# One load queue, a rewritten opening order, and earlier slots for turns and gates, in a recurrence-plus-feed-forward kernel

## The chip, the cores and the metric

The kernel runs on one core of one Trainium2 chip. The metric is the device time of one execution in microseconds (us). Runs are taken in rounds beside runs of the kernel before on the same chip. A ratio is the mean time of one kernel's fast runs over the mean of the other's fast runs of the same rounds. It is therefore not quite the ratio of the two medians that are quoted with it. The brackets after a ratio are its 95% interval.

The kernel before took 401.45 us (three runs, 400.94 to 402.1).

## The reference, cut to what matters

```python
def _attn_ref(x, f_logit, lower_bound):            # x, f_logit: (4, 6144, 256)
    sig = 1.0 / (1.0 + np.exp(-f_logit))
    f = lower_bound + (1.0 - lower_bound) * sig
    i = 1.0 - f
    for t in range(S):                              # a gated recurrence along the sequence
        h = f[:, t] * h + i[:, t] * x[:, t]
        y[:, t] = h

def _moe_ref(x, w1, w2, w_out):                     # 24576 tokens, 256 -> 1024 -> 256
    return np.maximum(x @ w1, x @ w2) @ w_out
```

The kernel uses max(a, b) = a + relu(b - a). The hidden products use the difference of the two weights, and the part that is linear in `x @ w1` becomes one 256x256 product (`w13` in the code).

## The kernel before: the parts that matter

There are 48 blocks of 512 tokens. Blocks 0 to 3 (the "opening") are loaded as plain rows and transposed on TensorE. All later blocks go another way, in chunks of two. POOL starts a DMA that casts both inputs to bf16 in DRAM ("cast"). SyncE (SP) then starts DMA transposes of them into SBUF ("turn"). Then ScalarE (ACT) makes the gate and VectorE (DVE) the drive, the forget factors and the scans ("gate").

```python
    def turn_dma(c):                                  # chunk c = blocks 4+2c, 5+2c
        for s, name in enumerate(("fs", "xs")):
            t = ttpool.tile([P, KC, CB * TB], BF16, name=("fT", "xT")[s])
            turned[c, s] = t
            nc.sync.dma_start_transpose(out=t[:], in_=spare[c % NS, name][:])

    def cast_behind(c):
        if c + 1 < NCH:
            last = CB * TB - 1                        # POOL waits here for the transpose fT
            nc.gpsimd.tensor_copy(out=held[:], in_=turned[c, 0][:, KC - 1, last : last + 1])
            cast(c + 1)

    def gate(j):                                      # ACT
        ...
        nc.scalar.activation(out=us[j][:], in_=part(j, 0), func=AF.Sigmoid, scale=-1.0)

    def drive(j):                                     # DVE; forget_half and scan_half follow
        nc.vector.tensor_tensor(out=vs[j][:], in0=us[j][:], in1=part(j, 1), op=ALU.mult)
```

The order of the opening is a hand-made list of items. Each item is one instruction group. Its suffix names the engine: `.a` ACT, `.v` DVE, `.p` POOL. `H` is a hidden product, `R` its relu, `P` a projection step, `G`/`V`/`F`/`S` are gate, drive, forget and scan, `TU`/`TV` transposes on TensorE, `D`/`SC` weight difference and scale, `warm` filler matmuls, and `CA` the first cast and turn. `O` copies a finished output out; the other letters round, transpose and apply weights. In the list of loads, `f0a` is half a of block 0's gate input, `x0a` that of its other input, and `w13` quarter 3 of w1 (not the product of the same name). Each engine works through its own part of the list in order.

```python
    LOADS = """
    f0a x0a f0b w13 w23 x0b w12 w22 wo3 w11 w21 w10 wo2 w20 f1a x1a wo1 f1b wo0 x1b
    f2a x3b f3a x2a f2b x2b f3b x3a
    """
    PLAN = """
    warm1 keeps_T G0a RW3.p V0a keeps TU0a D30.p F0a1.v G0b warm1 TV0a warm3 TU0b
    F0a0.a S0a1 F0b0.a warm1 TW3 S0a0 F0b1.a KW3.a V0b SC30.a D31.p RW2.v D20.p
    ...
    P150 R27.a H22a P160 H23a R22.a S3b0 H25b H25a H20b H23b H20a R25.a R23.v R20.v
    P120 O11.v O10.a
    """
    turn_of = {(4, 1): 1, (6, 0): 2}
    turn_of |= {(NP + c * CB - 3, 5): c for c in range(3, NCH)}
    gate_of = {(3, 3): 4, (4, 0): 5, (5, 0): 6, (5, 5): 7, (6, 6): 8, (7, 3): 9}
    gate_of |= {(b - 2, 5): b for b in range(10, NBLK)}
    ...
        for k, name in enumerate(LOADS.split()):
            load_item(name, nc.scalar if k in (1, 3) else nc.sync)   # x0a alone goes to ACT's queue
            if k == 0:
                nc.sync.dma_start(out=lbr[:], in_=lower_bound...)
    ...
        for j in range(3, NBLK + 1):
            for fc in range(FC):                      # slot (j, fc), eight in a block
                if j < NBLK:
                    hidden(j, fc)                     # two 128x512 matmuls, then relu(j, fc) on ACT
                project(j - 1, fc)                    # five 128x256 matmuls
                if fc == 0 and j > 3: store(j - 2, 1) # copy on DVE, then the store's issue on SP
                if fc == 4 and j < NBLK: store(j - 1, 0)
                ...
                if (j, fc) in gate_of:  ...           # gate, drive, forget, scan of a later block
                if (j, fc) in turn_of:  ...           # turn of a chunk, cast of the next
```

Slot (0) of block j needs the relus of slots 0 to 4 of block j-1.

Of the kernel before, what the change touches and what calls it, by code (L numbers as in the profile page):

```python
# [12 lines left out]
P = 128  # L13
# [3 lines left out]
def kernel(  # L17
# [13 lines left out]
    nc = tc.nc  # L31
# [26 lines left out]
    midpool = ctx.enter_context(tc.tile_pool(name="mid", bufs=2))  # L58
    ypool = ctx.enter_context(tc.tile_pool(name="ypool", bufs=4))
    rpool = ctx.enter_context(tc.tile_pool(name="rpool", bufs=3 * FC))  # L60
    opool = ctx.enter_context(tc.tile_pool(name="opool", bufs=6))
    lastpool = ctx.enter_context(tc.tile_pool(name="last", bufs=2))
    PS = bass.MemoryType.PSUM
    ps_d = ctx.enter_context(tc.tile_pool(name="ps_d", bufs=5, space=PS))
# [28 lines left out]
        ffs[j] = nffpool.tile([P, KC, TB], BF16, name="nff")  # L93
        ys[j] = ypool.tile([P, KC, TB], BF16, name="y")

    def load(j, s, q0, q1, eng=nc.sync):
        src = (f_logit, x)[s]
        eng.dma_start(
            out=ins[j][s][:, q0:q1, :],
            in_=src[0, j * TB + q0 * P : j * TB + q1 * P, :].rearrange(  # L100
                "(q p) d -> p q d", p=P
            ),
        )
# [128 lines left out]
    def relu(j, fc, on_dve=False):  # L232
        rt = rpool.tile([P, TB], BF16, name="rt")
        rts[j, fc] = rt
        if on_dve:
            nc.vector.tensor_relu(out=rt[:], in_=dts[j, fc][:])
        else:
            nc.scalar.activation(out=rt[:], in_=dts[j, fc][:], func=AF.Relu)  # L238

    def hidden(j, fc):  # L240
        dts[j, fc] = ps_d.tile([P, TB], FP32, name="dT")
        for kc in range(KC):
            nc.tensor.matmul(  # L243
                dts[j, fc][:],
                lhsT=wd[:, kc, unit(fc)],
                rhs=ys[j][:, kc, :],
                start=(kc == 0),
                stop=(kc == KC - 1),
            )
        relu(j, fc)  # L250

    pos = {}
# [90 lines left out]
    def wout_load(k):  # L343
        nc.sync.dma_start(
            out=won[:, 2 * k : 2 * k + 2, :],
            in_=moe_w_out[k * QF : (k + 1) * QF, :].rearrange("(q p) c -> p q c", p=P),
        )
# [90 lines left out]


    LOADS = """  # L440
    f0a x0a f0b w13 w23 x0b w12 w22 wo3 w11 w21 w10 wo2 w20 f1a x1a wo1 f1b wo0 x1b
    f2a x3b f3a x2a f2b x2b f3b x3a
    """
    PLAN = """
    warm1 keeps_T G0a RW3.p V0a keeps TU0a D30.p F0a1.v G0b warm1 TV0a warm3 TU0b
    F0a0.a S0a1 F0b0.a warm1 TW3 S0a0 F0b1.a KW3.a V0b SC30.a D31.p RW2.v D20.p
    warm5 TV0b S0b0 D21.p D11.p S0b1 TW2 KW2.v SC31.a H07a SC21.v H06a RO3.a warm3
    H07b H06b SC20.a R07.a W133 H05a D10.v H05b R06.a RW0.a H04b SC10.v P071 SC11.v
    H04a RW1.p P060 P061 R05.v D00.v H02b RO2.p TW0 R04.a H02a R02.a G1a D01.p TW1
    RO1.p P040 H03b KW0.v KW1.a SC00.v P051 SC01.v H03a V1a R03.a W132 P070 TU1a  # L450
    P041 H01b H00b H01a TV1a G1b F1a1.v H00a P030 P020 P031 R00.a RO0.p W131 TU1b
    P021 F1a0.v S1a1 W130 R01.a P050 F1b0.a S1a0 G2a P010 KL1.a V1b TV1b KL0.a
    F1b1.v P000 TU2a H11a H14a H16a S1b1 G3a P001 S1b0 P011 L01 F2a1.a H11b V2a H14b
    L00 F2a0.v H17a G2b O01.a R14.v TV2a L11 R11.a H16b L10 TU2b S2a0 R16.a G3b P140
    H17b S2a1 H12a H12b P141 F2b1.v P111 R17.a H13b V2b H13a H15a R12.a F2b0.v H15b
    TV2b P170 TU3b CA H10b H10a R15.a R13.v P110 F3b1.a TU3a R10.a F3b0.a S2b1 P121
    P130 S2b0 V3a P151 H21a H21b F3a1.a P161 H26b H26a R21.a TV3a P100 V3b H24a
    F3a0.v R26.a P131 S3a1 H24b H27b P171 H22b TV3b R24.a H27a P101 O00.a S3a0 S3b1
    P150 R27.a H22a P160 H23a R22.a S3b0 H25b H25a H20b H23b H20a R25.a R23.v R20.v
    P120 O11.v O10.a  # L460
    """

    engines = {"a": nc.scalar, "v": nc.vector, "p": nc.gpsimd}

    def load_item(name, eng=nc.sync):
        if name[0] == "w":
            k = int(name[2])
            if name[1] == "o":
                wout_load(k)
            elif name[1] == "1":  # L470
                weight_load(k, w1n, moe_w1)
            else:
                weight_load(k, w2n, moe_w2)
        else:
            half = 2 * "ab".index(name[2])
            load(int(name[1]), "fx".index(name[0]), half, half + 2, eng)

    outs = []

# [5 lines left out]
    def issue(item):  # L485
        name, _, e = item.partition(".")
        eng, on_dve, on_act = engines.get(e), e == "v", e == "a"
        kind = name.rstrip("0123456789ab")
        arg = ["ab".index(c) if c in "ab" else int(c) for c in name[len(kind) :]]
        if kind == "warm":  # L490
            keep_warm(arg[0])
        elif name == "keeps_T":
            turn_bound()
        elif name == "keeps":
            keeps()
        elif kind in ("G", "V") and len(arg) == 2:
            (gate_nat if kind == "G" else drive_nat)(arg[0], 2 * arg[1], 2 * arg[1] + 2)
        elif kind in ("TU", "TV"):
            turn_pe(arg[0], "UV".index(kind[1]), arg[1])
        elif kind == "F" and len(arg) == 3:  # L500
            j, x, h = arg
            tok = slice(x * HB, (x + 1) * HB)
            forget(ffs[j][:, h, tok], uT[j, x][:, h, :], h, on_act)
        elif kind == "S" and len(arg) == 3:
            j, x, h = arg
            scan(j, h, x * HB, (x + 1) * HB, vT[j, x][:, h, :])
        elif kind == "RW":
            round_w1(arg[0], eng)
        elif kind == "RO":
            round_wout(arg[0], eng)  # L510
        elif kind == "D":
            diff(arg[0], arg[1], eng)
        elif kind == "SC":
            scale(arg[0], arg[1], on_dve)
        elif kind == "TW":
            turn_w1(arg[0])
        elif kind == "KW":
            keep_w1(arg[0], eng)
        elif kind == "W":
            linear_weights(int(name[3]))  # L520
        elif kind == "KL":
            keep_linear(arg[0], on_dve)
        elif kind == "H":
            hidden_half(*arg)
        elif kind == "R":
            relu(arg[0], arg[1], on_dve)
        elif kind == "P":
            pair_steps(arg[0], arg[2], [arg[1]])
        elif kind == "L":
            pair_steps(arg[0], arg[1], [FC, FC + 1])  # L530
        elif kind == "O":
            copy_out(arg[0], arg[1], on_act)
            outs.append(arg)
            send_pending()
        elif kind == "CA":
            nc.gpsimd.tensor_copy(out=held[:], in_=ins[2][0][:, 3, D - 1 : D])
            cast(0)
            turn_dma(0)
            cast_behind(0)
        else:  # L540
            raise ValueError(item)


    turn_of = {(4, 1): 1, (6, 0): 2}
    turn_of |= {(NP + c * CB - 3, 5): c for c in range(3, NCH)}
    gate_of = {(3, 3): 4, (4, 0): 5, (5, 0): 6, (5, 5): 7, (6, 6): 8, (7, 3): 9}
    gate_of |= {(b - 2, 5): b for b in range(10, NBLK)}

    with tc.manual_schedule():
        for j in range(NP):  # L550
            alloc_in(j)
        for k, name in enumerate(LOADS.split()):
            load_item(name, nc.scalar if k in (1, 3) else nc.sync)
            if k == 0:
                nc.sync.dma_start(out=lbr[:], in_=lower_bound.rearrange("(h p) -> h p", p=P))
        nc.vector.memset(warm[:], 0.0)  # L556
        make_identity(nc, ident[:])
        nc.vector.tensor_copy(out=ident_b[:], in_=ident[:])
        keep_warm(7)
        for item in PLAN.split():  # L560
            issue(item)
        assert not outs

        for j in range(3, NBLK + 1):
            for fc in range(FC):
                if j < NBLK:
                    hidden(j, fc)
                project(j - 1, fc)
                if fc == 0 and j > 3:
                    store(j - 2, 1)  # L570
                if fc == 4 and j < NBLK:
                    store(j - 1, 0)
                if j == NBLK and fc in (3, 5, 7):
                    if fc == 3:
                        store(j - 1, 0)
                    else:
                        store_row(j - 1, 1, (fc - 5) // 2)
                if (j, fc) in gate_of:
                    b = gate_of[j, fc]
                    gate(b)  # L580
                    drive(b)
                    for h in range(KC):
                        forget_half(b, h)
                        scan_half(b, h)
                if (j, fc) in turn_of:
                    turn_dma(turn_of[j, fc])
                    cast_behind(turn_of[j, fc])
# [30 lines left out]
```

## Time and profile before

| what | before |
|---|---|
| time, us | 401.45 (three runs) |
| span of the profiled run, us | 400.3 |
| PE busy | 98% |
| first hidden matmul's weights, us from the start | 10.12 |
| first hidden matmul of the loop (block 3) | 35.97 |
| steady loop block | 7.82 |

From the page of the kernel before, first the busy times (us, share of the span, instructions), then the chain that ended last (share of the span by engine):

```profile
PE 390.6 (98%) x2854; PEld 276.1 (69%) x2854; DVE 251.5 (63%) x365; ACT 273.8 (68%) x452; POOL 42.3 (11%) x83
...
PE 85%; DMA 7%; DVE 4%; ACT 1%; SPq 1%; issue 1%; DVEq 0%; ACTq 0%
```

PE is what bounds the kernel, but a busy PE in this view is not PE at its peak. The chain in order of time is sharper. From a steady stretch of the kernel before (start us, us, what):

```profile
151.61 0.43 PE dT L243 x2
152.04 0.55 PE psO L263 x5
152.59 0.43 PE dT L243 x2
153.02 0.55 PE psO L263 x5
```

Two 128x512 matmuls take 0.43 us and five 128x256 ones 0.55 us, with nothing between them. Eight such pairs make 7.82 us, one block. The Trainium skill ("TensorE: Matmul & The Clock Gate", "Back-to-back issue gap") gives N/2.4 + 2.5 ns as the gap of an isolated matmul of N columns. From this formula I estimate 215.8 ns for 512 columns and 109.2 ns for 256, and 8 x (2 x 215.8 + 5 x 109.2) ns = 7.82 us for a block, which is what the trace shows. So I take the steady loop as it is, and look for time where PE waits. The waits of PE from 8 us on in the kernel before (us in total, times, longest):

```profile
PE psO L263 <- ACT rt L238: 1.7, 3, 1.0
PE dT L243 <- DVE y L147: 0.9, 1, 0.9
PE dT L124 <- ACT un L106: 0.8, 1, 0.8
PE dT L124 <- DVE vn L111: 0.6, 1, 0.6
PE psO L263 <- DVE rt L236: 0.5, 1, 0.5
```

The two at L124 are in blocks 0 and 2 of the opening, the others in loop blocks 3, 4, 7 and 9. The largest is a chain through four engines. From the timeline of the kernel before around loop blocks 6 and 7 (start us, us, engine, line, operation; in square brackets the idle time before it and what ended that):

```profile
64.31 0.67 DVE L312 COPY osb<-psO 128x512 f32<-128x512 f32 x1
...
65.01 0.33 SPq L316 DMA_DIRECT2D out_dram<-osb  x1
...
65.43 2.19 SPq L178 DMA_TRANSPOSE fT<-fs  x1
...
70.28 1.06 ACT L195 ACTIVATE u<-fT 128x1024 bf16<-128x1024 bf16 x1 [1.91 <-DMA fT<-fs]
...
71.25 2.20 ACT L238 ACTIVATE rt<-dT 128x512 bf16<-128x512 f32 x4
...
71.88 0.28 PE L263 MATMUL psO<-wob,rt 128*128 128x256 bf16 x1 [0.99 <-ACT rt L238]
```

Read it upwards. PE waits for a relu, which stands on ACT behind the gate of block 8. That gate waited 1.91 us for the transpose, which SP issued only after a store, whose copy stood on DVE behind the scans of block 7.

### The profile page before, as it was taken

The page shows a single profiled execution, that of the slowest core. Times are in us where ns is not written, and L with a number is a line of the kernel's source. Part 1 is how long each engine was busy: PE and PEld are TensorE (multiplying, and loading weights), DVE is VectorE, ACT ScalarE, POOL GpSimd, SP SyncE. Part 2 cuts the span into 40 slices and gives each one's busy share as a digit, 9 for nine tenths or more (in the row PEclk, how much of TensorE's full clock was granted, in tenths as well). Part 3 has the DMA queues.
Part 4 walks back from the last instruction along what each step waited for, and adds up shares of the span by engine and source line. Part 5 has one row for each costly group of instructions (what it writes and reads, how often), then busy time and mean ns, then how long its engine had stood idle before and what let it go on. Part 6 is the DMA issues. An engine that isn't in the chain of part 4 may idle for free.

```text
span 400.3 us, 7223 instructions
## 1 busy us (share of the span) xinstructions
PE 390.6 (98%) x2854; PEld 276.1 (69%) x2854; DVE 251.5 (63%) x365; ACT 273.8 (68%) x452; POOL 42.3 (11%) x83
## 2 busy tenths in 40 slices
PE   8999999999999999999999999999999999999996
PEld 3887677666777677766776677667776777667764
DVE  4976775738576567657755765676576567657622
ACT  5777675766766676677667667766766776676661
POOL 2511010110111010110110110110201101100000
PEclk9999999999999999999999999999999999999999
DMA  8989996989999999999999999998999999895122
GB/s 259 349 213 202 216 212 145 195 192 218 233 219 218 205 181 219 200 192 218 195 189 222 195 200 212 184 234 186 180 213 209 196 223 194 191 215 146 52 99 87
DMA packets 125110, 79.12 MB, mean 198 GB/s; under 512 B 94226, under 2 KB 101652, under 8 KB 125076
## 3 DMA queue, kind: packets, MB, share of 16 engines
q1 hardware_dynamic: 112836, 55.33, 54.4%
q0 software_dynamic: 11968, 23.07, 35.5%
q8 instruction: 22, 0.36, 0.4%
q10 hardware_dynamic: 272, 0.26, 0.2%
q14 instruction: 12, 0.10, 0.1%
HBM read 53.48 MB, written 48.23 MB: 254 GB/s over the span
## 4 chain that ended last, share of the span: by engine, by line
PE 85%; DMA 7%; DVE 4%; ACT 1%; SPq 1%; issue 1%; DVEq 0%; ACTq 0%
PE psO L263 47%; PE dT L243 35%; DVE y L147 2%; DMA fn<-in_f_logit_dram 2%; PE dT L223 2%; DMA won<-in_moe_w_out_dram 1%; DMA w2n<-in_moe_w_dram 1%; DMA fT<-fs 1%; DMA xT<-xs 1%; ACT u L195 1%; DVE v L199 1%; SPq L178 1%; DVE ff L136 1%; PE dT L124 0%; DVE osb L312 0%
## 5 line engine op out<-in xcount | busy, mean ns | idle before, releaser
L238 ACT ACTIVATE rt<-dT 128x512 bf16<-128x512 f32 x379 | 221.9, 596 | 105.9 <-PE dT L243 103.0
L263 PE MATMUL psO<-wob,rt 128*128 128x256 bf16 x1536 | 231.5, 273 | 2.2 <-ACT rt L238 1.7
L263 PEld LDWEIGHTS <-rt 128*128 128x128 bf16 x1536 | 149.9, 98 | 98.1 <-ACT rt L238 2.5
L243 PE MATMUL dT<-y,wd 128*128 128x512 bf16 x720 | 214.3, 379 | 0.9 <-DVE y L147 0.9
L147 DVE TENSOR_TENSOR_SCAN y<-ff,y,v 128x512 bf16<-128x512 bf16 x82 | 105.3, 1284 | 2.9
L199 DVE TENSOR_TENSOR v<-u,xT 128x1024 bf16<-128x1024 bf16 x44 | 30.4, 692 | 102.3 <-ACT u L195 86.6
L312 DVE COPY osb<-psO 128x512 f32<-128x512 f32 x92 | 62.1, 679 | 28.6 <-PE psO L263 28.6
L243 PEld LDWEIGHTS <-wd 128*128 128x128 bf16 x720 | 70.5, 98 | 8.2
L263 PE MATMUL psO<-w,y 128*128 128x256 bf16 x384 | 72.6, 273 | 0.0
L195 ACT ACTIVATE u<-fT 128x1024 bf16<-128x1024 bf16 x44 | 46.2, 1049 | 4.2 <-DMA fT<-fs 4.2
L184 POOL CAST held<-fT 128x1 f32<-128x1 bf16 x21 | 10.1, 479 | 288.6 <-DMA fT<-fs 288.6
L263 PEld LDWEIGHTS <-y 128*128 128x128 bf16 x384 | 37.5, 98 | 4.4
L136 DVE TENSOR_SCALAR ff<-u,nom 128x512 bf16<-128x512 bf16 x88 | 29.8, 338 | 0.0
L223 PE MATMUL dT<-y,wd 128*128 128x256 bf16 x96 | 14.7, 273 | 0.0
L168 POOL DMA_DIRECT2D fs<-in_f_logit_dram x22 | 12.3, 558 | 2.8 <-issue 2.6
L168 POOL DMA_DIRECT2D xs<-in_x_dram x22 | 12.1, 550 | 0.0
L147 DVE TENSOR_TENSOR_SCAN y<-nff,y,dT 128x256 bf16<-128x256 bf16 x14 | 9.7, 734 | 2.1 <-PE dT L124 1.8
L223 PEld LDWEIGHTS <-wd 128*128 128x128 bf16 x96 | 9.1, 98 | 1.4 <-issue 0.2
L111 DVE TENSOR_TENSOR vn<-un,xn 128x512 bf16<-128x512 bf16 x8 | 6.0, 755 | 5.2 <-ACT un L106 3.3
L428 PE MATMUL psO<-warm 128*128 128x512 bf16 x21 | 7.6, 494 | 1.2 <-DVE warm L556 1.2
L106 ACT ACTIVATE un<-fn 128x512 bf16<-128x512 f32 x8 | 5.0, 628 | 4.5 <-DMA fn<-in_f_logit_dram 4.5
L147 DVE TENSOR_TENSOR_SCAN y<-ff,v 128x512 bf16<-128x512 bf16 x6 | 7.3, 1225 | 0.2
(41 smaller groups left out, 54.7 us busy)
## 6 DMA issues: line engine op xcount, KB each, us to landing
out_dram<-osb SPq DMA_DIRECT2D x95, 256.0 KB, 2.8
fs<-in_f_logit_dram POOLq DMA_DIRECT2D x22, 512.0 KB, 6.1
xs<-in_x_dram POOLq DMA_DIRECT2D x22, 512.0 KB, 9.1
fn<-in_f_logit_dram SPq DMA_DIRECT2D x8, 256.0 KB, 7.3
xn<-in_x_dram SPq DMA_DIRECT2D x7, 256.0 KB, 6.7
w1n<-in_moe_w_dram SPq DMA_DIRECT2D x4, 256.0 KB, 5.4
w2n<-in_moe_w_dram SPq DMA_DIRECT2D x4, 256.0 KB, 5.6
won<-in_moe_w_out_dram SPq DMA_DIRECT2D x4, 256.0 KB, 6.0
```

Source lines behind the costliest of these rows:

```text
L136: nc.vector.tensor_scalar(out=o, in0=i, scalar1=nom[:, h : h + 1], scalar2=1.0, op0=ALU.mult, op1=ALU.add)
L147: nc.vector.tensor_tensor_scan(out=ys[j][:, h, t0:t1], data0=ffs[j][:, h, t0:t1], data1=v, initial=initial, op0=ALU.mult, op1=ALU.add,)
L168: nc.gpsimd.dma_start(out=spare[c % NS, name][:], in_=src[b, k * TB : (k + CB) * TB, :], max_dma_last_dim=4096,)
L184: nc.gpsimd.tensor_copy(out=held[:], in_=turned[c, 0][:, KC - 1, last : last + 1])
L195: nc.scalar.activation(out=us[j][:], in_=part(j, 0), func=AF.Sigmoid, scale=-1.0)
L199: nc.vector.tensor_tensor(out=vs[j][:], in0=us[j][:], in1=part(j, 1), op=ALU.mult)
L223: nc.tensor.matmul(dts[j, fc][:, tok], lhsT=wd[:, kc, unit(fc)], rhs=ys[j][:, kc, tok], start=(first and kc == 0), stop=(not first and kc ...
L238: nc.scalar.activation(out=rt[:], in_=dts[j, fc][:], func=AF.Relu)
L243: nc.tensor.matmul(dts[j, fc][:], lhsT=wd[:, kc, unit(fc)], rhs=ys[j][:, kc, :], start=(kc == 0), stop=(kc == KC - 1),)
L263: nc.tensor.matmul(ps, lhsT=lhsT, rhs=rhs, start=start, stop=stop, skip_group_check=True)
L312: nc.vector.tensor_copy(out=osbs[j, g][:], in_=pos[j, g, 0][:])
L428: nc.tensor.matmul(idle[:].rearrange("p r d -> p (r d)"), lhsT=warm[:, 0:P], rhs=warm[:], start=True, stop=True,)
```

## The change

The intent is to fill PE's waits in the opening and in the first loop blocks. The diff, cut to its core:

```diff
-    opool = ctx.enter_context(tc.tile_pool(name="opool", bufs=6))
+    opool = ctx.enter_context(tc.tile_pool(name="opool", bufs=8))
...
-    f0a x0a f0b w13 w23 x0b w12 w22 wo3 w11 w21 w10 wo2 w20 f1a x1a wo1 f1b wo0 x1b
-    f2a x3b f3a x2a f2b x2b f3b x3a
+    f0a x0a f0b w13 w23 x0b w12 w22 wo3 w10 w20 w11 wo2 w21 f1a x1a wo0 f1b x1b wo1
+    f2a f2b x2a x2b f3 x3
...                                        (the whole PLAN is replaced; its first and last lines:)
-    warm1 keeps_T G0a RW3.p V0a keeps TU0a D30.p F0a1.v G0b warm1 TV0a warm3 TU0b
+    G0a RW3.p keeps_T keeps V0a TU0a D31.p warm3 TV0a D30.p G0b F0a0.v warm4 TU0b
...
-    P150 R27.a H22a P160 H23a R22.a S3b0 H25b H25a H20b H23b H20a R25.a R23.v R20.v
-    P120 O11.v O10.a
+    TV3b R21.a P121 P110 S3a0 H22 R27.a S3b1 P130 R24.a R22.a S3b0 H23 P131 R23.a
+    H25 P140 O10.v P141 R25.a O11.v CA
...
-            nc.gpsimd.tensor_copy(out=held[:], in_=ins[2][0][:, 3, D - 1 : D])
+            nc.gpsimd.tensor_copy(out=held[:], in_=ins[2][1][:, 3, D - 1 : D])
...                                        (after the first cast and turn, now the last item:)
+            send_pending()
...
-    turn_of = {(4, 1): 1, (6, 0): 2}
-    turn_of |= {(NP + c * CB - 3, 5): c for c in range(3, NCH)}
-    gate_of = {(3, 3): 4, (4, 0): 5, (5, 0): 6, (5, 5): 7, (6, 6): 8, (7, 3): 9}
-    gate_of |= {(b - 2, 5): b for b in range(10, NBLK)}
+    turn_of = {(3, 5): 1, (5, 2): 2, (7, 0): 3}
+    turn_of |= {divmod(FC * (NP + c * CB - 3) - 3, FC): c for c in range(4, NCH)}
+    gate_of = {(3, 1): 4, (3, 6): 5, (4, 5): 6, (5, 3): 7, (6, 3): 8, (7, 1): 9}
+    gate_of |= {(b - 2, 4): b for b in range(10, NBLK)}
...
-        for k, name in enumerate(LOADS.split()):
-            load_item(name, nc.scalar if k in (1, 3) else nc.sync)
-            if k == 0:
-                nc.sync.dma_start(out=lbr[:], in_=lower_bound...)
+        nc.scalar.dma_start(out=lbr[:], in_=lower_bound...)
+        for name in LOADS.split():
+            load_item(name)
```

The hidden products of block 2 also become whole ones (512 columns) instead of two halves. Block 3's two inputs are loaded as one DMA each (`f3`, `x3`) instead of two.

More of the change, by code (lines that the diff above doesn't have):

```diff
@@ L94, in alloc_in, with load @@
         ys[j] = ypool.tile([P, KC, TB], BF16, name="y")
-    def load(j, s, q0, q1, eng=nc.sync):
+    def load(j, s, half=None):
         src = (f_logit, x)[s]
-        eng.dma_start(
+        q0, q1 = (0, NQ) if half is None else (2 * half, 2 * half + 2)
+        nc.sync.dma_start(
             out=ins[j][s][:, q0:q1, :],
@@ L238, in relu, with hidden_whole @@
             nc.scalar.activation(out=rt[:], in_=dts[j, fc][:], func=AF.Relu)
-    def hidden(j, fc):
+    def hidden_whole(j, fc):
         dts[j, fc] = ps_d.tile([P, TB], FP32, name="dT")
@@ L249, in hidden @@
             )
+    def hidden(j, fc):
+        hidden_whole(j, fc)
         relu(j, fc)
@@ L440 @@
     LOADS = """
-    f0a x0a f0b w13 w23 x0b w12 w22 wo3 w11 w21 w10 wo2 w20 f1a x1a wo1 f1b wo0 x1b
-    f2a x3b f3a x2a f2b x2b f3b x3a
+    f0a x0a f0b w13 w23 x0b w12 w22 wo3 w10 w20 w11 wo2 w21 f1a x1a wo0 f1b x1b wo1
+    f2a f2b x2a x2b f3 x3
     """
     PLAN = """
-    warm1 keeps_T G0a RW3.p V0a keeps TU0a D30.p F0a1.v G0b warm1 TV0a warm3 TU0b
-    F0a0.a S0a1 F0b0.a warm1 TW3 S0a0 F0b1.a KW3.a V0b SC30.a D31.p RW2.v D20.p
-    warm5 TV0b S0b0 D21.p D11.p S0b1 TW2 KW2.v SC31.a H07a SC21.v H06a RO3.a warm3
@@ L448 @@
-    H07b H06b SC20.a R07.a W133 H05a D10.v H05b R06.a RW0.a H04b SC10.v P071 SC11.v
-    H04a RW1.p P060 P061 R05.v D00.v H02b RO2.p TW0 R04.a H02a R02.a G1a D01.p TW1
-    RO1.p P040 H03b KW0.v KW1.a SC00.v P051 SC01.v H03a V1a R03.a W132 P070 TU1a
-    P041 H01b H00b H01a TV1a G1b F1a1.v H00a P030 P020 P031 R00.a RO0.p W131 TU1b
-    P021 F1a0.v S1a1 W130 R01.a P050 F1b0.a S1a0 G2a P010 KL1.a V1b TV1b KL0.a
-    F1b1.v P000 TU2a H11a H14a H16a S1b1 G3a P001 S1b0 P011 L01 F2a1.a H11b V2a H14b
@@ L454 @@
-    L00 F2a0.v H17a G2b O01.a R14.v TV2a L11 R11.a H16b L10 TU2b S2a0 R16.a G3b P140
-    H17b S2a1 H12a H12b P141 F2b1.v P111 R17.a H13b V2b H13a H15a R12.a F2b0.v H15b
-    TV2b P170 TU3b CA H10b H10a R15.a R13.v P110 F3b1.a TU3a R10.a F3b0.a S2b1 P121
-    P130 S2b0 V3a P151 H21a H21b F3a1.a P161 H26b H26a R21.a TV3a P100 V3b H24a
-    F3a0.v R26.a P131 S3a1 H24b H27b P171 H22b TV3b R24.a H27a P101 O00.a S3a0 S3b1
-    P150 R27.a H22a P160 H23a R22.a S3b0 H25b H25a H20b H23b H20a R25.a R23.v R20.v
@@ L460 @@
-    P120 O11.v O10.a
+    G0a RW3.p keeps_T keeps V0a TU0a D31.p warm3 TV0a D30.p G0b F0a0.v warm4 TU0b
+    D21.p F0a1.v S0a1 S0a0 V0b F0b1.a warm1 TW3 F0b0.a RW0.p warm5 TV0b RW2.v S0b1
+    D01.p KW3.a TW2 SC31.a SC30.a KW2.a S0b0 RO3.a H06a H07a D20.v SC21.a warm3 H06b
+    SC20.v H07b D00.v W133 RW1.v R07.a TW0 H04b H04a RO2.p H05a R06.a P071 SC00.v
+    H05b P070 P061 D10.p TW1 SC01.a KW0.v R05.a R04.v H01a KW1.v H00a H00b H01b P040
+    P050 P060 G1a P041 SC10.v V1a W132 R01.a D11.p TU1a RO0.p SC11.a P051 TV1a R00.a
@@ new lines @@
+    H02a F1a1.v F1a0.a RO1.p H03b S1a1 P011 G1b H02b S1a0 P010 H03a R02.a W130 V1b
+    P001 R03.a TU1b H17a F1b1.v P000 TV1b H15a F1b0.a S1b1 S1b0 G2a H16a P031 P030
+    P021 G2b W131 KL1.v TU2a F2a0.a P020 H17b H15b KL0.v H16b L01 L11 R17.a TU2b
+    H10a H10b R16.a V2a R15.v F2a1.v H11b O01.a P161 H11a TV2a F2b0.a H12b P151 L10
+    P171 V2b H12a R11.a F2b1.v R10.a S2a1 TV2b S2a0 G3b P150 R12.a S2b1 G3a L00 S2b0
+    H13a V3b TU3b O00.a H13b P101 R13.a F3b1.v H14a P160 F3b0.v H14b P100 P170 H20
@@ L461, with load_item @@
+    H26 V3a TU3a P111 F3a1.v H21 R14.a H27 R20.a F3a0.v R26.a TV3a S3a1 P120 H24
+    TV3b R21.a P121 P110 S3a0 H22 R27.a S3b1 P130 R24.a R22.a S3b0 H23 P131 R23.a
+    H25 P140 O10.v P141 R25.a O11.v CA
     """
     engines = {"a": nc.scalar, "v": nc.vector, "p": nc.gpsimd}
-    def load_item(name, eng=nc.sync):
-        if name[0] == "w":
-            k = int(name[2])
-            if name[1] == "o":
-                wout_load(k)
-            elif name[1] == "1":
-                weight_load(k, w1n, moe_w1)
-            else:
-                weight_load(k, w2n, moe_w2)
-        else:
-            half = 2 * "ab".index(name[2])
-            load(int(name[1]), "fx".index(name[0]), half, half + 2, eng)
+    def load_item(name):
+        if name[:2] == "wo":
+            wout_load(int(name[2]))
+        elif name[0] == "w":
+            w, src = ((w1n, moe_w1), (w2n, moe_w2))[int(name[1]) - 1]
+            weight_load(int(name[2]), w, src)
+        else:
+            half = ("ab".index(name[2]),) if len(name) == 3 else ()
+            load(int(name[1]), "fx".index(name[0]), *half)
@@ L523, in issue @@
         elif kind == "H":
-            hidden_half(*arg)
+            (hidden_half if len(arg) == 3 else hidden_whole)(*arg)
         elif kind == "R":
@@ L551 @@
             alloc_in(j)
-        for k, name in enumerate(LOADS.split()):
-            load_item(name, nc.scalar if k in (1, 3) else nc.sync)
-            if k == 0:
-                nc.sync.dma_start(out=lbr[:], in_=lower_bound.rearrange("(h p) -> h p", p=P))
+        nc.scalar.dma_start(out=lbr[:], in_=lower_bound.rearrange("(h p) -> h p", p=P))
+        for name in LOADS.split():
+            load_item(name)
         nc.vector.memset(warm[:], 0.0)
```

## The prediction

> **What bounds the kernel now.** TensorE: PE is busy 390.6 of 400.3 us (98%, the page's first part) at full granted clock, and 85% of the chain of waits. In the steady loop the timeline shows a 512-token block every 7.82 us, with no PE wait from 95 to 385 us (list of waits). 48 x 7.82 = 375 us; the other 25 are about 10 us before the first hidden matmul (10.12), 4 after the last matmul, 7 of transposes and linear weights, and bubbles. Those on PE, from the timeline:
> - 9.0: 0.65 us for block 0's second drive; 0.65 us of fillers at 10.6;
> - 21.2: 0.82 us for the gate of block 2, whose load landed 7.4 us after issue (loads run at 345 to 350 GB/s until 22 us);
> - 36.7: 0.52 us for relu R20 on DVE;
> - 45.0: 0.90 us for block 4's second scan (its gate is issued at slot (3,3));
> - 70.9 and 88: 0.99 and 0.68 us for relus behind a gate on ACT that waits for a transpose (1.9 and 2.3 us). On SP that transpose stands behind a store, whose copy stands on DVE behind an earlier block's scans (copies at 64.3 and 80.3, transposes at 65.4 and 81.5).
>
> **What the change does.**
> 1. x0a moves from ACT's queue to SP, lower_bound the other way: same bytes. The Trainium skill ("DMA: Bandwidth & Descriptors", "Issuing engines are not separate DMA queues") says another issuer saves only issue time, here 0.37 to 0.48 us. f0a up to 0.3 us earlier, x0a 0.4 later: about nothing, since PE's start waits for weights and x0b, sixth in both orders.
> 2. Block 3's half loads become whole: same bytes, two issues fewer, and after block 2's. The first cast waits for x2b, landing about 23.1 (f2b before: 24.0): first transpose 0.5 to 1 us earlier.
> 3. Opening order. Block 2's hidden products are whole: 16 x 0.215 us for 32 x 0.109: nothing. About 0.9 us more ready work stands before block 2's first transpose: fills the 0.82. R20 goes to ACT, earlier: the 0.52 mostly goes. Hidden products start within 0.5 us of before. Two more fillers, in waits.
> 4. Slots. Gates of blocks 4 to 9 move earlier, block 4 by two slots (2 us): the 0.90 goes. Turns 1 to 3 move earlier, turn 3 ahead of gate 9: the 0.99 and 0.68 go. In the steady loop turns come a block earlier and gates a slot; PE waits for nothing there, so no gain.
> 5. opool 8: slack for stores behind the first transpose.
>
> **Sum.** 0.8 + 0.5 + 0.9 + 1.7 = 3.9 us, all on the critical path. I allow 0.9 us for new bubbles in the rewritten opening. **398.4 us**, 8 in 10 within **396.4 to 401.2**. Faster by over 2%: 0.01; within 2%: 0.97; slower by over 2%: 0.02. PE's work is not shortened, so 2% (8 us) would need more than all bubbles.
>
> **What would show it.** PE busy still about 390 us, span 3 us shorter; no PE wait for scan L147 near 45; no ACT wait for fT near 70 and 86; transposes 2 and 3 issued over 5 us before their gates; loop's first matmul near 34.7 us (36.1 before); steady block still 7.82 us.
>
> **What would make it wrong.** The new order starving PE (a late relu, scan or weight scale in an in-order queue); earlier casts and transposes colliding with block 3's loads; a transpose waiting on SP for its cast and holding stores until copies stop.

## The result, and the profile after

The changed kernel took 397.27 us (four runs, 397.12 to 397.79), beside 401.75 us for the kernel before. The ratio is 0.9894 [0.9875, 0.9913], so it is about 4.3 us faster. The page of the changed kernel, busy times and the chain that ended last:

```profile
PE 387.6 (98%) x2793; PEld 275.0 (70%) x2840; DVE 251.2 (63%) x366; ACT 273.3 (69%) x451; POOL 39.2 (10%) x83
...
PE 95%; DMA 1%; DVE 1%; issue 1%; SPq 1%; DVEq 0%
```

(The counts of PE and PEld differ: some 50 matmul records are missing from this trace. The weight loads are the safer count.) The chain is now PE for 95% of the span instead of 85%. The waits of PE from 8 us on, all that is left:

```profile
PE dT L126 <- DVE vn L113: 0.9, 1, 0.9
PE dT L225 <- DVE wd L388: 0.2, 1, 0.2
```

The bubbles after 13.5 us are gone. To see where the time came from, I take the start of the first hidden weight load of each loop block in both traces:

| stretch (us) | before | after | gain |
|---|---|---|---|
| start to loop block 3 | 35.97 | 35.90 | 0.07 |
| block 3 | 8.51 | 7.82 | 0.69 |
| block 4 | 8.87 | 7.82 | 1.05 |
| block 7 | 8.99 | 7.89 | 1.10 |
| block 9 | 8.85 | 7.82 | 1.03 |
| blocks 5, 6, 8, 10 | 31.28 | 31.28 | 0 |
| blocks 11 to 46, 36 of them | 281.52 | 281.52 | 0 |
| start of block 47 to the end | 16.27 | 15.55 | 0.72 |
| span | 400.26 | 395.60 | 4.66 |

The traced execution of before took 402.07 us, somewhat above the medians, that of after 397.38, so this table explains 4.7 us where the runs differ by 4.3.

Three things stand out. The long rewrite of the opening brought the loop forward by only 0.07 us. The loop blocks brought 3.9 us. And the end of the program, which no line of the change seems to touch, brought 0.7 us. (Block 7's 7.89 us has 0.07 us over 7.82; no listed wait of PE accounts for it.)

**The gates.** The timeline of the changed kernel around the same gate, block 8's:

```profile
58.92 3.09 SPq L180 DMA_TRANSPOSE fT<-fs  x1
...
65.67 1.06 ACT L197 ACTIVATE u<-fT 128x1024 bf16<-128x1024 bf16 x1 [2.04 <-DMA fT<-fs]
...
66.63 3.02 ACT L240 ACTIVATE rt<-dT 128x512 bf16<-128x512 f32 x6
...
67.72 0.71 PE L268 MATMUL psO<-wob,rt 128*128 128x256 bf16 x5
```

The transpose is issued 6.5 us earlier (4.7 us, if counted from the start of block 6). In the trace of before its cast had landed at 58.27, and the transpose was issued 7.16 us later, behind the store. Here it was issued at 58.92, 0.02 us after its cast landed, so no store holds it any more. But the gate moved earlier too, from slot (6,6) to (6,3), and still waits 2.04 us. PE shows no wait for it: its matmuls have no bracket. Six relus follow back to back, and no matmul of block 7 waits for one. So the wait that I had predicted to vanish is still there, in a place where it costs nothing. Whether the earlier transpose or the gate's place in its block is what cured the loss is open at this point.

**The first hidden matmul** starts later, not earlier. From the timeline, the transposes of block 0's second drive, before and after:

```profile
8.29 1.26 DVE L111 TENSOR_TENSOR vn<-un,xn 128x512 bf16<-128x512 bf16 x1 [0.53 <-DMA xn<-in_x_dram]
...
9.61 0.40 PE L124 MATMUL dT<-ident_b,vn 128*128 128x128 bf16 x4 [0.65 <-DVE vn L111]
```

```profile
8.80 1.20 DVE L113 TENSOR_TENSOR vn<-un,xn 128x512 bf16<-128x512 bf16 x1 [0.96 <-DMA xn<-in_x_dram]
...
10.06 0.40 PE L126 MATMUL dT<-ident_b,vn 128*128 128x128 bf16 x4 [0.91 <-DVE vn L113]
```

The load x0b, on which everything here hangs, landed at 8.26 before and at 8.71 after, although f0a landed earlier (4.22 before, 3.60 after). The drive itself is slow here too: 1.26 and 1.20 us, where 13 of the 14 other such drives in the two traces took 0.67 to 0.69. A weight difference ran on POOL beside it for 0.71 and 0.66 us. The Trainium skill ("SBUF — State Buffer", "Who interferes with whom") says that a DVE instruction with two SBUF inputs contends with a POOL instruction that reads SBUF. These traces agree, though no run tested it, and neither PLAN avoids it.

**The end.** The last store landed at 398.64 of 400.26 us before and at 394.69 of 395.60 after, so 1.62 and 0.91 us ahead of the end. SP's waits in the last 3 to 4 us, before and after:

```profile
SPq L613 <- DMA out_dram<-row: 1.2, 2, 1.0
```

```profile
SPq L614 <- DMA out_dram<-row: 0.5, 1, 0.5
```

At the end SP passes a list of waits. In the trace of before it reaches the wait that this last store ends as the third, at 398.66, and passes six more by 399.37. In the trace of after it reaches it as the ninth, at 394.71. By then the others are done, while the store was still under way. The semaphores that each DMA signals when it completes explain this (they are in the compiled programs' lists, and the traces show the same). The DMAs issued by SP and ACT take their completion semaphores in turn from a set of eight, and SP's waits at the end go through this set in its order. The kernel before has 170 such DMAs and its last two stores sit on numbers 0 and 1. The changed kernel has 168 (block 3's two loads fewer) and they sit on 6 and 7.

### The profile page after: what moved, and what is told of

The parts are those of the page before. It is cut to its first block, busy times and chain, and to the rows that moved or that the text cites. A ratio compares the mean times of both kernels' runs of the same rounds, so it can differ in the third digit from the quotient of the medians.

```text
span 395.6 us, 7146 instructions
## 1 busy us (share of the span) xinstructions
PE 387.6 (98%) x2793; PEld 275.0 (70%) x2840; DVE 251.2 (63%) x366; ACT 273.3 (69%) x451; POOL 39.2 (10%) x83
## 4 chain that ended last, share of the span: by engine, by line
PE 95%; DMA 1%; DVE 1%; issue 1%; SPq 1%; DVEq 0%
PE psO L268 53%; PE dT L245 39%; PE dT L225 2%; DMA xn<-in_x_dram 1%; PE dT L126 1%; SPq L100 0%; PE psO L413 0%; DVE vn L113 0%; SPq L344 0%; DVE y L149 0%; DVE wd L388 0%; DVE wdf L380 0%; DVE row L332 0%; PE dT L396 0%; DVEq L113 0%
## 5 line engine op out<-in xcount | busy, mean ns | idle before, releaser
L245 PE MATMUL dT<-y,wd 128*128 128x512 bf16 x690 | 208.8, 379 | 2.2
L245 PEld LDWEIGHTS <-wd 128*128 128x128 bf16 x736 | 72.0, 98 | 8.8
L186 POOL CAST held<-fT 128x1 f32<-128x1 bf16 x21 | 6.7, 319 | 278.9 <-DMA fT<-fs 278.9
L225 PE MATMUL dT<-y,wd 128*128 128x256 bf16 x64 | 10.1, 273 | 0.3 <-DVE wd L388 0.2
L225 PEld LDWEIGHTS <-wd 128*128 128x128 bf16 x64 | 5.8, 98 | 1.4 <-issue 0.4
```

Source lines behind the costliest of these rows:

```text
L225: nc.tensor.matmul(dts[j, fc][:, tok], lhsT=wd[:, kc, unit(fc)], rhs=ys[j][:, kc, tok], start=(first and kc == 0), stop=(not first and kc ...
L245: nc.tensor.matmul(dts[j, fc][:], lhsT=wd[:, kc, unit(fc)], rhs=ys[j][:, kc, :], start=(kc == 0), stop=(kc == KC - 1),)
```

## The experiments

All kernels gave correct results. Each had five rounds. The table has the medians (us) of the kernel and of the kernel before in the same rounds, then landmarks of the profiled run.

| run | time / before | ratio [95%] | first hidden | loop start | block 3 | 4 | 5 | 7 | 9 | last landing to end |
|---|---|---|---|---|---|---|---|---|---|---|
| (before) | 401.45 | | 10.12 | 35.97 | 8.51 | 8.87 | 7.82 | 8.99 | 8.85 | 1.62 |
| (after) | 397.27 / 401.75 | 0.9894 [0.9875, 0.9913] | 10.58 | 35.90 | 7.82 | 7.82 | 7.82 | 7.89 | 7.82 | 0.91 |
| slots_only | 398.59 / 401.33 | 0.9930 [0.9917, 0.9944] | 10.37 | 35.27 | 8.51 | 7.82 | 7.82 | 7.82 | 7.82 | 1.61 |
| opening_only | 401.22 / 401.33 | 1.0004 [0.9988, 1.0019] | 10.70 | 36.03 | 7.82 | 8.87 | 7.82 | 8.65 | 9.76 | 0.91 |
| turns_only | 399.36 / 401.33 | 0.9950 [0.9938, 0.9962] | 10.41 | 35.48 | 8.51 | 8.88 | 7.82 | 7.82 | 7.82 | 1.61 |
| gates_only | 403.99 / 401.33 | 1.0068 [1.0049, 1.0086] | 10.07 | 35.88 | 8.51 | 7.82 | 10.47 | 10.41 | 8.17 | 1.62 |
| min_slots | 398.22 / 401.25 | 0.9926 [0.9913, 0.9938] | 10.26 | 35.40 | 8.51 | 7.82 | 7.82 | 7.82 | 7.82 | 1.61 |
| steady_old | 397.62 / 401.25 | 0.9906 [0.9891, 0.9921] | 11.12 | 36.45 | 7.82 | 7.82 | 7.82 | 7.82 | 7.82 | 0.92 |
| halves3 | 398.10 / 401.92 | 0.9909 [0.9892, 0.9927] | 11.08 | 36.42 | 7.82 | 7.82 | 7.82 | 7.82 | 7.82 | 1.62 |
| x0a_back | 396.88 / 401.92 | 0.9882 [0.9864, 0.9900] | 10.30 | 35.59 | 7.82 | 7.82 | 7.82 | 7.82 | 7.82 | 0.91 |
| scan_swap | 397.54 / 401.92 | 0.9892 [0.9872, 0.9912] | 10.04 | 34.92 | 7.82 | 7.82 | 7.82 | 7.82 | 7.82 | 0.91 |
| x0a_swap | 397.17 / 401.92 | 0.9891 [0.9873, 0.9908] | 10.22 | 35.58 | 7.82 | 7.82 | 7.82 | 7.82 | 7.82 | 0.90 |
| queue_only | 401.51 / 401.25 | 1.0007 [0.9994, 1.0021] | 11.10 | 36.38 | 8.50 | 8.87 | 7.82 | 8.71 | 8.62 | 1.63 |
| small_edits | 398.81 / 401.25 | 0.9939 [0.9927, 0.9952] | 10.18 | 37.18 | 8.03 | 7.82 | 7.82 | 7.82 | 7.82 | 0.90 |

### slots_only and opening_only: which half of the change gains

slots_only is the kernel before with the four new lines of `turn_of` and `gate_of`. opening_only is the changed kernel with the four old ones.

> The kernel before with the changed kernel's slots of turns and gates alone (old opening, old queues, opool of 6). Theory S (all that the slots can cure lies in blocks 4, 7 and 9, which lost 1.05, 1.17 and 1.03 us in the trace of before): loop blocks 4 to 9 last 7.82 us each, block 3 still 8.5 (the R20 wait stays), first hidden matmul still at 10.1, time 3.2 us shorter than before, ratio 0.992. Rival O (the slots only work with the new opening, whose earlier first cast and larger store pool feed them): under 1.5 us shorter, with waits for the first transposes on ACT and PE.

> The changed kernel with the old slots of turns and gates. Theory S: the loop starts within 0.2 us of before (35.9), block 3 lasts 7.8 instead of 8.5, blocks 4, 7 and 9 again lose 1.0 to 1.2 us each; and the end of the program is 0.7 us shorter than in before, as in the changed kernel; so about 1.4 us shorter than before, ratio 0.9965. Rival O: about 3 us shorter, the losses of blocks 4, 7 and 9 smaller than 0.5 us each.

slots_only gave 0.9930, close to the expected 0.992. Blocks 4, 7 and 9 are cured, with the old opening and the old store pool of 6. Rival O falls. opening_only gave 1.0004, not the expected 0.9965. Its landmarks are as expected at the loop start, in block 3, in block 4 and at the end, but block 7 lost 0.83 us and block 9 lost 1.94 (9.76 - 7.82), instead of 1.0 to 1.2 each. ACT waited 3.2 us in block 9 for the transpose: it landed at 86.31, in before at 86.36, although block 8 had begun about 1 us earlier than in before. So the new opening gains 0.7 us in block 3 and 0.7 at the end, and with the old slots it gives 0.9 of that back in block 9. Why this transpose did not come earlier along with the loop I did not settle. One profile was taken of it.

### turns_only, gates_only and min_slots: the transpose or the gate's place

```diff
 turns_only (on before)
-    turn_of = {(4, 1): 1, (6, 0): 2}
-    turn_of |= {(NP + c * CB - 3, 5): c for c in range(3, NCH)}
+    turn_of = {(3, 5): 1, (5, 2): 2, (7, 0): 3}
+    turn_of |= {(NP + c * CB - 3, 5): c for c in range(4, NCH)}
 gates_only (on before)
-    gate_of = {(3, 3): 4, (4, 0): 5, (5, 0): 6, (5, 5): 7, (6, 6): 8, (7, 3): 9}
+    gate_of = {(3, 1): 4, (3, 6): 5, (4, 5): 6, (5, 3): 7, (6, 3): 8, (7, 1): 9}
 min_slots = turns_only, and
-    gate_of = {(3, 3): 4, ...
+    gate_of = {(3, 1): 4, ...
```

> The kernel before with turns 1, 2 and 3 alone moved to the new slots; all gates and the later turns as before. Theory T (the transposes came late): no wait of ACT for fT at gates 8 and 10, blocks 7 and 9 last 7.82, block 4 still loses 1.05: time 2.2 us shorter than before, ratio 0.9945. Rival G (what cures is the gate's slot in its block, since ACT then has the rest of the block to catch up; the changed kernel still waits 1.0 and 2.0 us for fT with no loss on PE): blocks 7 and 9 still lose over 0.5 us each.

> The kernel before with the gates of blocks 4 to 9 alone moved to the new slots; turns and later gates as before. Theory T: the gates now stand before their transposes have landed, ACT waits 2 us or more for fT at gates 6 and 8, and PE loses time there: block 4 is cured (1.05 us) but the total is no more than 1 us shorter than before, perhaps longer, ratio 0.9975 to 1.003. Rival G: about 2.5 to 3.2 us shorter, ratio about 0.993, in spite of long waits for fT on ACT.

> The kernel before with four slots moved and nothing else: turns 1, 2, 3 as in the changed kernel and the gate of block 4 from (3,3) to (3,1). Theory (these four are all that the slots cure; the other gates and all of the steady loop add nothing): loop blocks 4 to 10 last 7.82 us each, block 3 8.51, ratio to before 0.9925, as the run with all slots (0.993). Rival (the other gates matter too, since a gate late in its block leaves ACT no time to catch up): some block from 5 to 9 still loses over 0.3 us.

turns_only cured blocks 7 and 9 whole, at the old gate slots (0.9950, expected 0.9945). PE's waits from 36 to 120 us are those of blocks 4 and 3 alone, and from 40 to 95 us ACT waits for PE and for no transpose:

```profile
PE dT L243 <- DVE y L147: 0.9, 1, 0.9
PE psO L263 <- DVE rt L236: 0.5, 1, 0.5
```

```profile
ACT rt L238 <- PE dT L243: 16.2, 39, 1.4
```

gates_only made the kernel 2.7 us slower, worse than the range that theory T named. Blocks 5 and 7 lost 2.65 and 2.59 us. ACT's and PE's waits in gates_only, from 36 to 120 us:

```profile
ACT u L195 <- DMA fT<-fs: 9.4, 3, 4.0
```

```profile
PE psO L263 <- ACT rt L238: 3.6, 5, 2.1
```

So it was the lateness of the transpose that cost time, and the gate's place in its block can absorb about 2 us of waiting but not 4: gate 8 waited 1.91 us at (6,6) in before, and block 7 lost 1.17; it waited 2.04 us at (6,3) in the changed kernel, and no matmul waited. So rival G has a part of the truth, but it is not what cured the loss in turns_only. min_slots shows that four moves are enough: turns 1 to 3 and the gate of block 4. (Whether turn 1 is needed was not tested; in before no gate waits for it.) It gave 0.9926, the same as all slots (0.9930), and every block from 4 on took 7.82 us. Its one wait on PE from 36 to 120 us is the relu R20, which belongs to the opening:

```profile
PE psO L263 <- DVE rt L236: 0.7, 1, 0.7
```

In all six traces with the old PLAN and R20 on DVE, block 3 took 8.50 or 8.51 us. In all seven with the new PLAN it took 7.82. In small_edits, with the old PLAN but R20 on ACT, it took 8.03, so the change of engine brings most of it.

### steady_old: the new slots of the steady loop

```diff
-    turn_of |= {divmod(FC * (NP + c * CB - 3) - 3, FC): c for c in range(4, NCH)}
-    gate_of |= {(b - 2, 4): b for b in range(10, NBLK)}
+    turn_of |= {(NP + c * CB - 3, 5): c for c in range(4, NCH)}
+    gate_of |= {(b - 2, 5): b for b in range(10, NBLK)}
```

> The changed kernel with the old slots in the steady loop (turn 4 and later one block later, gate of block 10 and later one slot later). Theory: PE waits for nothing there, so the block stays at 7.82 and the time is the changed kernel's, ratio to before 0.989 to 0.990. Rival (the earlier turns keep a reserve that the old slots lack): a block over 7.9 us somewhere after block 10, or ratio over 0.991.

The ratio, 0.9906, lies a little outside the expected 0.989 to 0.990. Its interval, 0.9891 to 0.9921, holds most of that range and also the rival's values over 0.991. The traces decide: from block 11 to the end it took 297.08 us, the changed kernel 297.07, and no block took over 7.9. min_slots and slots_only differ in the same steady slots (and some gates), and both took 297.79. Its profiled run lost 0.55 us before the loop, where x0b landed late (below). The steady slots add nothing.

### halves3: the end of the program

```diff
-    f2a f2b x2a x2b f3 x3
+    f2a f2b x2a x2b f3a f3b x3a x3b
```

> The changed kernel with block 3's two inputs loaded as four halves again, at the same place in the load order. What was seen: the two executions' last row stores landed 1.62 us (before) and 0.91 us (after) ahead of the end of the span; the compiled lists show that completion semaphores are dealt out in turn from eight, that the last two stores sit on numbers 0 and 1 in before and on 6 and 7 in after, and that at the end SyncE goes through them in order. Theory N (two issues fewer moved the last stores to the end of that list): the gap from the last landing to the end is 1.6 us again, the loop starts as in the changed kernel, time 0.7 us longer than the changed kernel's, ratio to before 0.991. Rival (the larger pool or the queues shortened the end): gap 0.9 us, time as the changed kernel's, ratio 0.9894.

The gap from the last landing to the end is 1.62 us again, from nothing but two more DMAs early in the program. SP's wait at the end is again that of before:

```profile
SPq L614 <- DMA out_dram<-row: 1.2, 2, 1.0
```

Over all fourteen traces: the seven kernels with 170 such DMAs have their last two stores on semaphores 0 and 1, and a gap of 1.61 to 1.63 us; the seven with 168 have them on 6 and 7, and a gap of 0.90 to 0.92. The store pool cannot be the cause, since small_edits has the pool of 6 and the short end. Theory N is shown. The time, 0.9909, is as expected. Its profiled run also started the loop late (36.42), so the ratio alone would not carry it.

### x0a_back and queue_only: one load queue or two

x0a_back, on the changed kernel; queue_only makes the opposite move on the kernel before.

```diff
-        nc.scalar.dma_start(out=lbr[:], in_=lower_bound...)
-        for name in LOADS.split():
-            load_item(name)
+        for k, name in enumerate(LOADS.split()):
+            load_item(name, nc.scalar if k == 1 else nc.sync)
+            if k == 0:
+                nc.sync.dma_start(out=lbr[:], in_=lower_bound...)
```

> The changed kernel with x0a issued from ACT's queue and lower_bound from SP again. Theory Q (one queue delays what follows: x0b landed at 8.7 to 8.8 instead of 8.3 to 8.6, the first hidden matmul began at 10.6 to 10.7 instead of 10.1 to 10.4): f0a lands later (4.2 to 4.4), f0b earlier (5.2 to 5.3), x0b before 8.6, first hidden matmul at 10.1 to 10.4, loop start about 0.3 us earlier than the changed kernel's 35.9, ratio to before 0.9885. Rival R (that is scatter between executions): first hidden matmul at 10.6 as in the changed kernel, ratio 0.9894.

> The kernel before with both first loads on SP's queue and lower_bound on ACT's, nothing else. Theory Q: f0a lands at 3.5 to 3.6 instead of 4.2 to 4.5, f0b later than 5.6 instead of 5.2 to 5.3, x0b at 8.7 or later, first hidden matmul about 0.35 us later than with two queues (10.1 to 10.4), loop start at 36.0 or later; ratio 1.000 to 1.002. Rival R (scatter): x0b at 8.3 to 8.6, ratio 1.000. A gain (ratio under 0.999) would say that the early f0a helps after all, as the change intended.

One profile each would not settle this, so I put together all fourteen traces, which have one arrangement or the other:

| | f0a landed | f0b landed | x0b landed | first hidden, range | mean |
|---|---|---|---|---|---|
| two queues, 8 traces | 4.09 to 4.22 | 5.16 to 5.68 | 8.26 to 8.59 | 10.07 to 10.41 | 10.24 |
| one queue, 6 traces | 3.51 to 3.61 | 5.69 to 6.70 | 8.14 to 9.26 | 10.04 to 11.12 | 10.77 |

(The expectations above give 4.2 to 4.5 for f0a on two queues; in seven of the eight traces that was a misreading of x0a, which landed at 4.42 to 4.55.) With one queue f0a lands about 0.5 us earlier, as the change must have intended, and so does x0a by 0.1 to 0.35 us (4.20 to 4.33). But the first hidden matmul does not wait for f0a. It waits for x0b and for weights, and x0b comes later in five of six traces, by up to 0.7 us beyond the latest of the two-queue traces. (lower_bound's small load moves the other way in the same edit; the two were not separated.) Its issue was only 0.17 us later (3.29 for 3.12). In time the effect is at the edge: queue_only 1.0007 [0.9994, 1.0021] and x0a_back 0.9882 beside the changed kernel's 0.9894 are both in the expected direction, and neither is separated by its interval. x0a_back has the lowest median of all kernels that ran (396.88 us). It beats the kernel before clearly and the changed kernel not clearly.

### scan_swap and x0a_swap: the order of two scans

```diff
-    ... TV0b RW2.v S0b1
+    ... TV0b RW2.v S0b0
-    D01.p KW3.a TW2 SC31.a SC30.a KW2.a S0b0 RO3.a H06a ...
+    D01.p KW3.a TW2 SC31.a SC30.a KW2.a S0b1 RO3.a H06a ...
```

x0a_swap has this edit and that of x0a_back.

> The changed kernel with the two scans of block 0's second half in the old order (channels 0 to 127 first), since the first matmul that needs them reads that half first. Theory P (in the changed order this matmul waits for both scans: 11.99 against 11.26 in before): it begins about 0.5 us earlier after the first hidden matmul, PE has only what the later weight scales leave to win, so 0.1 to 0.5 us off the loop start, ratio to before 0.9885. Rival: the weights of the next quarter, not the scan, bound there: loop start within 0.15 us of the changed kernel's, ratio 0.9894.

> Both edits, x0a back on ACT's queue and the old order of the two scans, on the changed kernel: a candidate that beats it. If theories Q and P both hold, first hidden matmul at 10.1 to 10.4 and loop start at 35.2 to 35.4, 0.5 to 0.7 us shorter than the changed kernel, ratio to before 0.988. If neither holds, ratio 0.9894 and loop start at 35.9.

The fair comparison is x0a_swap with x0a_back, whose x0b landed within 0.02 us of each other. The swap brought the waiting matmul from 11.71 to 11.36 us, as theory P said, and yet the loop started at 35.58 instead of 35.59. From the timelines of x0a_back and x0a_swap, 1.8 us later:

```profile
13.14 0.83 PE L225 MATMUL dT<-y,wd 128*128 128x256 bf16 x6 [0.17 <-DVE wd L388]
```

```profile
13.14 0.83 PE L225 MATMUL dT<-y,wd 128*128 128x256 bf16 x6 [0.36 <-DVE wd L388]
```

PE then waits for the scaled weights until the same moment, and the 0.35 us are gone. The rival was right. scan_swap itself has the earliest loop start of all (34.92), but also the earliest x0b (8.14), and its median (397.54) is no better than the others. The traced execution was by far its fastest (396.33). PE does not wait for scaled weights in it: a weight difference before them took 0.40 us on DVE, where it took 0.76 to 0.82 in the traces of after, x0a_back and x0a_swap. I take this for scatter and not for the swap; with one trace that is not shown.

### small_edits: can three edits do what the rewritten opening does

On before: all new slots, relu R20 on ACT, and whole loads of block 3.

```diff
-    f2a x3b f3a x2a f2b x2b f3b x3a
+    f2a x2a f2b x2b f3 x3
-    ... R25.a R23.v R20.v
+    ... R25.a R23.v R20.a
```

> The kernel before with three small edits, its own opening order and two queues kept, pool of 6: all new slots; block 3's inputs loaded whole, after block 2's; relu R20 on ACT. Theory (the long reordering of the opening is not what gains): blocks 3 to 10 last 7.82 to 7.9 each, gap from the last landing to the end 0.9 us, loop start at 35.3 to 36.0, so ratio to before 0.9885 to 0.990, as the changed kernel. Rival (the reordered opening is worth over half a us by itself): ratio 0.991 or more.

This missed: 0.9939. The end was short (0.90) and block 3 took 8.03 instead of 8.51, but the loop began at 37.18. From its timeline:

```profile
24.25 0.63 ACT L106 ACTIVATE un<-fn 128x512 bf16<-128x512 f32 x1 [2.96 <-DMA fn<-in_f_logit_dram]
...
25.68 0.38 PE L124 MATMUL dT<-ident_b,vn 128*128 128x128 bf16 x4 [1.77 <-DVE nff L136]
```

The old PLAN wants half a of block 3's gate input early (its load was the third of the last eight), and the whole load comes late. ACT works in order, so it stood for 2.96 us, and PE lost 1.77. The whole loads, and with them this way to the short end, need a PLAN that asks for block 3 later. This is one thing that the rewritten opening is good for. My rival reading ("the reordered opening is worth over half a us by itself") cannot be taken from this run, since the edit broke the order that it kept.

## Why the prediction was right, and where its steps were not

The predicted 398.4 us (396.4 to 401.2) held the measured 397.27. The reason was right in its main part: PE's own work stays the same, and what goes is PE's waits in loop blocks 3 to 9. The terms, as predicted and as measured:

- **Slots (step 4): right, and mis-sized.** I predicted 0.9 + 1.7 = 2.6 us from the waits of PE. The traces show 1.05 + 1.10 + 1.03 = 3.18 us, and min_slots shows that the four slots alone do it. I added up the waits listed for matmuls, and such a list comes out short. A wait is counted from the recorded end of the matmul before it, and that end is modelled. The traces record a matmul of 256 columns at 273 ns and one of 512 at 379 on average, while in the steady stretch one follows another after 109 and 216 ns. So I estimate that PE could have taken the next one about 0.16 us before the wait begins to count. With this the four waits (2.57 us) become 3.2, and blocks 4, 7 and 9 had lost 3.25 before. The length of a block against 7.82 us would have given the right size at once.
- **"No ACT wait for fT near 70 and 86": wrong.** Two waits (1.04 and 2.04 us at gates 6 and 8) are still there, as the gates moved forward too. They cost nothing. turns_only shows that the earlier transposes are what cures blocks 7 and 9, as I had said, and gates_only that moving the gates without them harms.
- **R20 (step 3): right.** 0.52 predicted as "mostly goes"; block 3 shrank by 0.69, which is 0.52 and the 0.16 of the point above.
- **The wait for block 2's gate (step 3): gone, but the sum that I put on it did not come.** Of the five traces with the old opening, its loads and two queues, before has this wait (0.82 us) and gates_only has it (0.66), where block 2's first gate load landed at 20.91 and 20.82. slots_only, turns_only and min_slots do not have it; there the load landed at 19.74 to 19.84. So I took for a fixed cost what comes and goes with the landings. The new opening has no such wait in any of its seven traces, although the load landed at 21.44 in the changed kernel. From the first hidden weights to the loop it took 25.29 to 25.36 us in six of the seven (24.88 in scan_swap), the old one 25.81 and 25.85 with the wait and 24.90 to 25.14 without. The changed kernel won 0.53 us there (25.32 for 25.85) and lost 0.46 before it, at the first hidden matmul. "Loop's first matmul near 34.7" was wrong: it was 36.0 (36.1 before).
- **Queues (step 1): wrong.** "About nothing" was a first hidden matmul 0.5 us later on average (10.77 for 10.24). x0a, which I expected 0.4 us later, landed earlier, and x0b later. I had looked at issue times, which moved 0.17 us for x0b, and not at landings.
- **First transpose "0.5 to 1 us earlier" (step 2): not in the changed kernel's trace, but on average.** There it was issued at 29.36 (29.20 before), with the first cast at 24.10 in both. Over the six traces with whole loads and the new opening it was issued at 27.93 to 29.36, 28.31 in the mean, and over the six with the old loads and opening at 28.38 to 29.70, 28.94 in the mean. It brought no time that shows.
- **"Two issues fewer" (step 2): the effect was missed.** I counted it as nothing. It took 0.7 us off the end of the program (halves3).
- **0.9 us for new bubbles: not needed after 13.5 us**, where the changed kernel has no PE wait.

The sum: I counted 0.8 + 0.5 + 2.6 us, less 0.9 for new bubbles, so 3.0. The traces show 0.07 + 0.69 + 3.18, and 0.72 at the end, so 4.66 (4.3 in the runs). The 0.7 us at the end, which I had not seen, make up for the missing gain of the opening (0.8 predicted). What is left is that slots and R20 were 0.8 us too small and the 0.9 us were not needed. The total lay in the range partly by such luck.

Left open: why x0b lands later and scatters more on one queue; whether the pool of 8 store buffers does anything (slots_only and min_slots gain fully with 6; the changed kernel was not run with 6); why block 9 of opening_only lost 1.94 us; and whether PE would start earlier if POOL left block 0's second drive alone.

## What to carry to other kernels

When the bounding engine waits for a long chain, follow it to the first instruction that merely stands in the wrong place of an in-order queue. Here, moving three transposes ahead of a store, and one gate by two slots, was worth 3 of the 4.3 us. A long rewrite of the opening did not bring the loop forward; what it gained came from one relu on another engine and from two DMAs fewer. Measure such losses by the length of a repeated unit against its undisturbed length, and take two or three traces before you count a wait for a load as a fixed cost. Look at the end of the program too: a DMA more or less, anywhere, can decide whether the last landing is waited for first or last.

## What the Trainium skill lacked or had wrong

- No page that I read says how the end of a program depends on the number of DMAs. Here completion semaphores go round a set of eight, and the end took 0.90 to 0.92 us after the last landing with the last stores on 6 and 7, and 1.61 to 1.63 us with them on 0 and 1.
- "TensorE: Matmul & The Clock Gate", "Back-to-back issue gap", calls N/2.4 + 2.5 ns the isolated gap and gives about 131 ns per matmul as sustained for N=512. This kernel sustains 0.43 us for two of 512 columns and 0.55 us for five of 256, each with its weight load. That is the isolated formula (215.8 and 109.2 ns), with no sign of 131.
- "DMA: Bandwidth & Descriptors", "Issuing engines are not separate DMA queues", says that another issuing engine saves only issue time. In the traces the choice also moved landings by more than the issue times: f0a, issued at 0.74 us in both arrangements, by about 0.5 us; f0b, issued 0.1 us later on one queue, from between 5.16 and 5.68 us to between 5.69 and 6.70; and the first hidden matmul by 0.5 us on average (8 traces against 6), with a wider scatter on one queue (10.04 to 11.12 against 10.07 to 10.41). The section also says that all DMAs share the same 16 engines and interleave, which fits such shifts, but it gives no size for them.
